# A float32r FFT and feed-forward kernel: the folds' casts and rests moved behind the operations on 1/std, and five groups of unread products between late steps

## The chip, the cores and the metric

The kernel runs on one core of a Trainium2 chip. The metric is the device time of one execution in microseconds, as a median over runs. Engines are named as the profile names them: PE is TensorE (its products), PEld its weight loads, DVE is VectorE, ACT is ScalarE, POOL is GpSimd, SP is SyncE, which issues most DMAs.

## The reference

An input of 8 x 3136 x 256 (batch, sequence, width) goes through a Fourier transform along the sequence and one along the width, of which the real part is kept; then comes a normalised two-layer feed-forward block with a residual:

```python
X = np.fft.fft(np.fft.fft(x, axis=1), axis=2)
y = X.real.astype(np.float32)
mu, var = np.mean(y, -1), np.mean((y - mu) ** 2, -1)
yn = (y - mu) / np.sqrt(var + 1e-06) * g_ln
out = y + np.maximum(yn @ w_ch1, 0.0) @ w_ch2      # 256 -> 1024 -> 256
```

## The kernel before, in words

The real part of the transform has a symmetry between rows k and N - k, so the kernel works on half of the rows, 1567 a batch and two single ones, and makes the outputs of a row and its mirror together. The rows of all eight batches stand in one line, cut into chunks of 256, 49 in all (the last one wider). The mean is taken out by the transform, and 1/std, a factor of a row, is applied at the end.

**The main loop** (L820 to L828) takes a chunk c in 8 steps, s = 8c to 8c + 7; step s handles 128 of the 1024 hidden columns. All large products are float32r, split in a high and a low part, three products for one. A step has

- `moe1_a(s)`: 6 products of 256 columns on PE (L354) into the two PSUM buffers tagged `ab`; then ACT copies one half (`asb`, L359) and DVE makes the sum and difference `h` (L360, L361). The buffer is free once L361 has read it, and `moe1_a(s + 2)` needs it;
- `moe1_b(s - 1)`: `h_hi` on ACT (L368) and its rest `h_lo` on DVE (L369, two operands in SBUF);
- `moe2(s - 3)`: 12 products of 256 columns (L404) that add up in PSUM (`acc`).

Around this stand two lists, `late[s]`, recorded between `moe1_a(s)` and `moe2(s - 3)`, and `after[s]`, recorded behind them. The order of each engine's instructions is the order in which they are recorded; DMAs aside, no scheduler moves them. In the lists are

- for each chunk, at step 8c + 5: `step2` (the second stage of the transform for a coming chunk, L309: 8 products of 98 columns or so, or 16, with copies on ACT and a rest on DVE, L334), and `residual` (the transform along the width, L428, 8 products as the profile counts them);
- then the norm of chunk c: `std(c)` on ACT at step 8c + 9, `inverse_std(c)` on DVE (L467, L468, L469, L471: four operations on a tile of 128 x 2) at 8c + 10, that is at a step 8k + 2 (for the first two chunks one step later each), and `finish` (L477, L479) at 8c + 11 and 8c + 12;
- for each batch b, seven folds i, ahead of the first stage of the transform of that batch. `steps1[b]` holds the step d of each: `fold_zw` (L207, L208) and `fold_eo` (L213, L214) on POOL at d - 7 and d - 6, the cast `fold_hi` on ACT (L219) at d - 4, the rest `fold_lo` on POOL (L225, it needs the cast) at d - 3, and `step1` at d: 3 products of 512 columns on PE (L262), a copy on ACT, a store. Most d are 6 or 7 above a multiple of 8. `step1_ends` adds a few small products (L237 to L241) per batch.

The last fold is due at step 318, while the loop runs to step 391, so POOL has nothing to do in the last fifth of the span.

```python
        for s in range(6, last):
            moe1_b(s - 1)
            moe1_a(s)
            for fn, args in late.get(s, ()):
                fn(*args)
            moe2(s - lag)
            for fn, args in after.get(s, ()):
                fn(*args)
```

Of the kernel before, what the change touches and what calls it, by code (L numbers as in the profile page):

```python
# [20 lines left out]
F32 = mybir.dt.float32  # L21
# [7 lines left out]
NB, N, D, FF = 8, 3136, 256, 1024  # L29
# [117 lines left out]
def tile_kernel(ctx: ExitStack, tc: tile.TileContext, x, g_ln, w1, w2, tu, tab, tz, ty, tw, out):  # L147
    nc = tc.nc
# [4 lines left out]
    psum = ctx.enter_context(tc.tile_pool(name="psum", bufs=1, space=bass.MemoryType.PSUM))  # L153
# [3 lines left out]
    w2_hi = moving.tile([128, 8, D], F32R, name="w2_hi")  # L157
# [4 lines left out]
    t1_hi = weights.tile([128, 128], F32R, name="t1_hi")  # L162
# [122 lines left out]
    def first_token(m):  # L285
        b, j = divmod(m, 8)
        return b * REG + max(gb[2 * j] - 2, 0)
# [305 lines left out]
    def finish_w2(n):  # L593
        _, e, f = conv.pop(f"w2_{n}")
        nc.vector.scalar_tensor_tensor(out=f, in0=f, scalar=2.0 ** -20, in1=e, op0=ALU.mult,
                                       op1=ALU.mult)
        return f
# [10 lines left out]
    def add(s, fn, *args):  # L608

        after.setdefault(s, []).append((fn, args))  # L610

    def add_late(s, fn, *args):

        late.setdefault(s, []).append((fn, args))

    first = {}
    for m in range(3, 64):
        s = 8 * (first_token(m) // CW) - 3
# [17 lines left out]
    for b in range(1, NB):  # L636
        need = 8 * (b * REG // CW) - 3
        at = steps1[b]
        ends_at = need - (58 if b > 1 else 30)
        add(need - 62 if b > 1 else ends_at - 7, ends, b)  # L640
        add(ends_at, step1_ends, b)
        for i, d in enumerate(at):
            d0, d = d, d - (b == 1)
            add(d - 7, fold_zw, b, i, nc.gpsimd)
            if b + 1 < NB:
                add(d - 5, load_x, b + 1, i)
            add(d - 6, fold_eo, b, i)
            add(d - 4, fold_hi, b, i)
            add(d - 3, fold_lo, b, i)
            add(d0, step1, b, i)  # L650
            add(d0, store1, b, i)
        add(at[-1] + 2, relayout, b)
    for c in range(LC):
        s = 8 * c + (5 if c > 1 else 6)
        add_late(8 * c + 9 + (c < 2), std, c)
        add_late(8 * c + 10 + (c < 2), inverse_std, c)
        for i in range(2):
            add(s, residual, c, i)
            add_late(s + 1, residual_e, c, i)
            add_late(s + i + 2, residual_y, c, i)  # L660
            add_late(8 * c + 11 + i, finish, c, i)
            add(8 * c + 11 + i, store_out, c, i)
    add_late(8 * LC - 2, singles)
    add_late(8 * LC + 7, std, LC)
    add_late(8 * LC, mixed)
# [15 lines left out]
    with tc.manual_schedule(engines={E.PE, E.Activation, E.DVE, E.Pool}):  # L681
        with tc.manual_schedule(engines={E.SP}):
# [91 lines left out]
            f = finish_w2(0)  # L774
# [8 lines left out]
            f = finish_w2(1)  # L783
# [18 lines left out]
            f = finish_w2(2)  # L802
# [51 lines left out]
```

## Time and profile before

| | us |
|---|---|
| median of 3 runs (lowest, highest) | 1012.02 (1011.04, 1012.07) |
| the profiled execution | 1010.0 |
| its span in the profile | 1008.2 |
| PE busy | 993.7 |
| DVE busy | 833.4 |
| ACT busy | 534.6 |
| POOL busy | 240.2 |
| PE idle ahead of L354 until DVE's L361 had ended, whole span | 6.4 in 13 pieces |

A row of a timeline gives the start and the length in us, the engine, the line, the operation, what it writes and reads, the shapes, how many instructions were merged, and in brackets the idle time before it with what ended it. A chain gives start, length, engine, tile and line of the pieces that followed each other without slack. The length of a product of PE (0.28 us for 256 columns) is longer than the distance from one start to the next, since products overlap; distances are what count.

### The profile page before, as it was taken

The numbers are of one execution on the slowest core, as the hardware profiler recorded it, in microseconds if no ns is written. First come the engines' busy times: TensorE is split into PE (matmuls) and PEld (weight loads), VectorE is DVE, ScalarE is ACT, GpSimd is POOL, SyncE is SP. The second block draws the span as 40 slices with busy tenths as digits, with TensorE's granted clock in tenths as the row PEclk, the third lists the DMA queues.
The fourth block names the chain that finished last, engine by engine and source line by source line (L and its number), as shares of the span: only waits on it lengthen the run. The fifth ranks groups of instructions, "written<-read, shape, count | busy, mean of one in ns | idle before, by whom it ended". The sixth has DMA issues, their size and how long they took to land.

```text
span 1008.2 us, 21760 instructions
## 1 busy us (share of the span) xinstructions
PE 993.7 (99%) x8289; PEld 969.7 (96%) x8289; DVE 833.4 (83%) x2190; ACT 534.6 (53%) x1416; POOL 240.2 (24%) x278
## 2 busy tenths in 40 slices
PE   9999999999999999999999999999999999999998
PEld 6799999999999999999999999999999999999998
DVE  6788887888888888887888887888888878887887
ACT  3655555554654555555555555554655555454553
POOL 1146433124212232312341125123322200000000
PEclk9999999999999999999999999999999999999999
DMA  9933352214221243121521242211311113100101
GB/s 344 262 145 125 107 161 81 79 58 136 86 93 54 75 141 100 55 74 62 170 74 64 84 129 93 90 58 64 116 43 43 53 43 96 43 23 22 43 22 43
DMA packets 41528, 92.10 MB, mean 91 GB/s; under 512 B 4176, under 2 KB 18704, under 8 KB 40528
## 3 DMA queue, kind: packets, MB, share of 16 engines
q1 hardware_dynamic: 40016, 88.87, 26.7%
q8 instruction: 66, 1.08, 0.5%
q0 software_dynamic: 320, 1.05, 0.3%
q10 hardware_dynamic: 1088, 0.79, 0.2%
q14 instruction: 38, 0.31, 0.1%
HBM read 50.32 MB, written 40.37 MB: 90 GB/s over the span
## 4 chain that ended last, share of the span: by engine, by line
PE 80%; DVE 13%; ACT 3%; DMA 2%; issue 2%; SPq 0%; ACTq 0%; DVEq 0%
PE acc L404 43%; PE ab L354 22%; PE ps L309 5%; DVE h_lo L369 4%; PE psy L428 4%; PE ps L262 3%; DVE h L361 2%; DVE h L360 2%; ACT h_hi L368 2%; DVE st L450 1%; DVE ve L468 1%; DVE ve L469 1%; DMA scratch<-s 1%; ACT s L265 1%; PE ps L255 1%
## 5 line engine op out<-in xcount | busy, mean ns | idle before, releaser
L404 PE MATMUL acc<-w_hi,h_lo 128*128 128x256 f32 x1568 | 435.7, 278 | 0.1
L404 PE MATMUL acc<-w_lo,h_hi 128*128 128x256 f32 x1568 | 435.5, 278 | 0.0
L404 PE MATMUL acc<-w_hi,h_hi 128*128 128x256 f32 x1568 | 435.5, 278 | 0.0
L368 ACT ACTIVATE h_hi<-h 128x512 fp32r<-128x512 f32 x392 | 249.7, 637 | 322.2 <-DVE h L361 322.1
L369 DVE SCALAR_TENSOR_TENSOR h_lo<-h,h_hi 128x512 fp32r<-128x512 f32 x392 | 287.5, 733 | 141.8 <-ACT h_hi L368 140.7
L404 PEld LDWEIGHTS acc<-w_hi,h_hi 128*128 128x128 f32 x1568 | 295.6, 189 | 0.0
L404 PEld LDWEIGHTS acc<-w_lo,h_hi 128*128 128x128 f32 x1568 | 295.1, 188 | 0.0
L404 PEld LDWEIGHTS acc<-w_hi,h_lo 128*128 128x128 f32 x1568 | 294.6, 188 | 0.4 <-DVE h_lo L369 0.3
L354 PE MATMUL ab<-ckl,w_hi 128*128 128x256 f32 x768 | 220.4, 287 | 6.5 <-DVE h L361 6.4
L354 PE MATMUL ab<-ckh,w_lo 128*128 128x256 f32 x768 | 213.9, 278 | 0.5 <-ACT ckh L330 0.4
L354 PE MATMUL ab<-ckh,w_hi 128*128 128x256 f32 x768 | 213.4, 278 | 0.0
L225 POOL TENSOR_TENSOR fl<-f,fh 128x512 fp32r<-128x512 f32 x49 | 64.1, 1307 | 527.1 <-ACT fh L219 478.4
L360 DVE TENSOR_TENSOR h<-asb,ab 128x256 f32<-128x256 f32 x384 | 158.3, 412 | 1.6 <-ACT asb L359 1.5
L361 DVE TENSOR_TENSOR h<-asb,ab 128x256 f32<-128x256 f32 x384 | 158.3, 412 | 0.0
L354 PEld LDWEIGHTS ab<-ckl,w_hi 128*128 128x128 f32 x768 | 144.3, 188 | 12.5 <-issue 7.6
L354 PEld LDWEIGHTS ab<-ckh,w_lo 128*128 128x128 f32 x768 | 144.7, 188 | 3.1 <-ACT ckh L330 0.5
L354 PEld LDWEIGHTS ab<-ckh,w_hi 128*128 128x128 f32 x768 | 144.8, 189 | 0.0
L359 ACT COPY asb<-ab 128x256 f32<-128x256 f32 x384 | 138.2, 360 | 10.8 <-PE ab L354 9.2
L265 ACT COPY s<-ps 128x508 f32<-128x508 f32 x56 | 32.8, 585 | 64.3 <-PE ps L262 50.5
L309 PE MATMUL ps<-tab_s,s 112*128 112x98 f32 (+1 forms) x512 | 65.5, 273 | 0.9 <-DMA s<-scratch 0.9
L309 PEld LDWEIGHTS ps<-tab_s,s 112*128 112x128 f32 x512 | 61.8, 191 | 1.4 <-PE pw L678 1.4
L330 ACT CAST ckh<-ps 128x392 fp32r<-128x392 f32 (+49 forms) x112 | 39.8, 356 | 29.5 <-PE ps L309 29.3
(108 smaller groups left out, 981.8 us busy)
## 6 DMA issues: line engine op xcount, KB each, us to landing
xs<-x SPq DMA_DIRECT2D x56, 512.0 KB, 4.1
out<-o SPq DMA_DIRECT2D x96, 256.0 KB, 2.0
scratch<-s SPq DMA_DIRECT2D x49, 256.0 KB, 2.3
s<-scratch SPq DMA_DIRECT2D x7, 1792.0 KB, 9.8
w1p_all<-w SPq DMA_DIRECT2D x8, 512.0 KB, 8.1
scratch<-s POOLq DMA_DIRECT2D x4, 256.0 KB, 6.1
s<-scratch SPq DMA_DIRECT2D x2, 448.0 KB, 5.6
s<-scratch SPq DMA_DIRECT2D x1, 896.0 KB, 12.0
```

The lines of the kernel that those rows point to most:

```text
L225: nc.gpsimd.tensor_tensor(out=lo, in0=f, in1=hi.bitcast(F32), op=ALU.subtract)
L265: nc.scalar.copy(s[:, :, :, :127], ps[:, :, :, :127])
L309: nc.tensor.matmul(ps[:, h, k0 - base:k1 - base], s2[b][:KP, g, 128 * h:128 * h + 128], tab_s[:, h, k0:k1], start=(h == 0 and g == 2 * j), ...
L330: nc.scalar.copy(hi, src)
L354: nc.tensor.matmul(pt, wt[wi][:, j, fs], ch[xi][:, j, :w], start=(n == 0), stop=(n == 2))
L359: nc.scalar.copy(asb[:, :w], pa)
L360: nc.vector.tensor_tensor(out=h[:, :w], in0=asb[:, :w], in1=pb, op=ALU.add)
L361: nc.vector.tensor_tensor(out=h[:, w:], in0=asb[:, :m], in1=pb[:, :m], op=ALU.subtract)
L368: nc.scalar.activation(h_hi, h, AF.Relu)
L369: nc.vector.scalar_tensor_tensor(out=h_lo, in0=h, scalar=0.0, in1=h_hi.bitcast(F32), op0=ALU.max, op1=ALU.subtract)
L404: nc.tensor.matmul(acc[c, i][:, side], hs[xi][:, h0:h0 + 128], ws[wi][:, f], start=(f == 0 and side == 0 and n == 0), stop=(f == 7 and n = ...
L428: nc.tensor.matmul(ps[:, j, :129 + j], ck[:, j], ty_s[:, j, :129 + j], start=(j == 0), stop=True, skip_group_check=True)
```

## The change

It has two parts.

The folds: `cast` is d - 4 as before, or d - 3 where d is 6 above a multiple of 8; the rest comes one step behind it. So in those folds the cast moves from `after[8k + 2]` to `after[8k + 3]` and the rest from there to `after[8k + 4]`. `inverse_std` stands in `late[8k + 2]`. 22 of the 49 folds move: 20 of the batches from 2 on, two of batch 1.

The products: a function `extra` allocates a PSUM tile of 128 x 2 x 256 under the tag `y` (one buffer, which step 2's second part, step 1 and two products of the last residual use too) and runs products of `t1_hi` (weights) on `w2_hi` into it. Nothing reads it. The index n counts blocks of 256 columns: width 1 is a product of 256 columns, width 2 one of 512. The groups stand behind what `after` holds for steps 326, 342, 350, 365 and 374.

```diff
-            add(d - 4, fold_hi, b, i)
-            add(d - 3, fold_lo, b, i)
+            cast = (d - 4, d - 3)[d % 8 == 6]
+            add(cast, fold_hi, b, i)
+            add(cast + 1, fold_lo, b, i)
...
+    def extra(s, widths):
+
+        ps = psum.tile([128, 2, D], F32, tag="y", name=f"extra{s}")
+        for n in widths:
+            nc.tensor.matmul(ps[:, :n], t1_hi, w2_hi[:, :n], start=True, stop=True)
+
+    for s, widths in ((326, (1,)), (342, (2,)), (350, (1, 1, 1)), (365, (1,)), (374, (2, 1))):
+        add(s, extra, s, widths)
```

On ACT, at steps 209 to 212, before (`fh5_5` is the cast of fold 5 of batch 5, due at step 214; `asb210` is the copy of step 210, `h_hi210` the high part of its h, `ve25` belongs to the std of chunk 25):

```order
L460 ACTIVATE ve25_8363<-ve25_8363 128x2
L368 ACTIVATE h_hi209_8410<-h209_8392 128x512
L359 COPY asb210_8421<-ab210_8414 128x256
L219 CAST fh5_5_8443<-f5_5_8377 128x512
L368 ACTIVATE h_hi210_8445<-h210_8422 128x512
L359 COPY asb211_8456<-ab211_8449 128x256
L368 ACTIVATE h_hi211_8481<-h211_8457 128x512
```

and in the change:

```order
L460 ACTIVATE ve25_8363<-ve25_8363 128x2
L368 ACTIVATE h_hi209_8410<-h209_8392 128x512
L359 COPY asb210_8421<-ab210_8414 128x256
L368 ACTIVATE h_hi210_8443<-h210_8422 128x512
L359 COPY asb211_8454<-ab211_8447 128x256
L219 CAST fh5_5_8476<-f5_5_8377 128x512
L368 ACTIVATE h_hi211_8479<-h211_8455 128x512
```

The cast stands two instructions later, behind the copy of step 211. The order on DVE is the same in both kernels. On POOL it differs at the two folds of batch 1 alone, where `fold_eo` of the next fold now stands ahead of the moved rest.

On PE, between steps 374 and 375, before (`acc46_1` is the sum of chunk 46, `ab375` the buffer of step 375):

```order
L404 MATMUL acc46_1_14429<-w2_lo_74,h_hi371_14437 128x256
L404 MATMUL acc46_1_14429<-w2_hi_73,h_hi371_14437 128x256
L354 MATMUL ab375_14555<-ckl46_13943,w1_hi_76 128x256
L354 MATMUL ab375_14555<-ckh46_13942,w1_lo_77 128x256
L354 MATMUL ab375_14555<-ckh46_13942,w1_hi_76 128x256
```

and in the change:

```order
L404 MATMUL acc46_1_14439<-w2_lo_74,h_hi371_14447 128x256
L404 MATMUL acc46_1_14439<-w2_hi_73,h_hi371_14447 128x256
L668 MATMUL extra374_14561<-w2_hi_73,t1_hi_78 128x512
L668 MATMUL extra374_14561<-w2_hi_73,t1_hi_78 128x256
L354 MATMUL ab375_14568<-ckl46_13951,w1_hi_76 128x256
```

Two products, of 512 and 256 columns, stand between the two steps. After 326, 342 and 350 the groups stand in the same way between L404 and L354; after 365 the group stands behind the residual's L428.

## The prediction

> **What bounds the kernel now.** First the page: TensorE (PE) is busy nearly the whole span. Then the groups of PE's instructions in the window that holds most of the loop (170 to 803 us): of the loop's two kinds of product only the first of L354 ever waits, always for the same operation.
>
> ```profile
> span 1008.2 us, 21760 instructions
> PE 993.7 (99%) x8289; PEld 969.7 (96%) x8289; DVE 833.4 (83%) x2190; ACT 534.6 (53%) x1416; POOL 240.2 (24%) x278
> ```
> ```profile
> L354 PE MATMUL ab<-ckl,w_hi 128*128 128x256 f32 x514 | 147.0, 286 | 4.2 <-DVE h L361 4.2
> ```
> ```profile
>   DVE h L361: 4.2, 8
> ```
>
> So in that window PE idles 4.2 us in 8 pieces, each ended by the second half of h (L361). The timeline of one of them, step 212 (time, length, engine, line), shows what VectorE (DVE) did before:
>
> ```profile
> 561.59 1.30 POOL L225 TENSOR_TENSOR fl<-f,fh 128x512 fp32r<-128x512 f32 x1 [12.50 <-ACT fh L219]
> ...
> 562.23 0.68 DVE L468 SCALAR_TENSOR_TENSOR ve<-ve 128x2 f32<-128x2 f32 x1
> ...
> 562.84 0.74 POOL L207 TENSOR_TENSOR zw<-xs 128x256 f32<-128x256 f32 x1
> ...
> 562.94 0.66 DVE L469 TENSOR_TENSOR ve<-ve 128x2 f32<-128x2 f32 x1
> 563.01 0.28 PE L354 MATMUL ab<-ckl,w_hi 128*128 128x256 f32 x1
> ...
> 563.63 0.57 DVE L471 SCALAR_TENSOR_TENSOR r<-ve 128x2 f32<-128x2 f32 x1
> ...
> 565.60 0.36 PE L354 MATMUL ab<-ckl,w_hi 128*128 128x256 f32 x1 [0.40 <-DVE h L361]
> ...
> 567.80 1.03 PE L309 MATMUL ps<-tab_s,s 112*128 112x98 f32 x8
> ```
>
> L468, L469 and L471 (of the 1/std) work on two columns and take 0.57 to 0.68 us each. The first two end 20 ns after a GpSimd (POOL) operation: L468 at 562.91, fl at 562.89; L469 at 563.60, zw at 563.58. Now the same place of a chunk whose rest comes one step later, at steps 67 to 69:
>
> ```profile
> 207.57 0.16 DVE L468 SCALAR_TENSOR_TENSOR ve<-ve 128x2 f32<-128x2 f32 x1
> ...
> 207.96 0.16 DVE L471 SCALAR_TENSOR_TENSOR r<-ve 128x2 f32<-128x2 f32 x1
> 208.16 0.69 DVE L369 SCALAR_TENSOR_TENSOR h_lo<-h,h_hi 128x512 fp32r<-128x512 f32 x1
> ...
> 208.99 1.30 POOL L225 TENSOR_TENSOR fl<-f,fh 128x512 fp32r<-128x512 f32 x1 [17.45 <-ACT fh L219]
> ...
> 212.28 1.17 DVE L369 SCALAR_TENSOR_TENSOR h_lo<-h,h_hi 128x512 fp32r<-128x512 f32 x1
> ```
>
> With POOL quiet L468 and L471 take 0.16 us each, and the cost falls on an h_lo instead (1.17 us; 0.69 alone). The chain of waits there (start, length, what) runs on PE alone, 0.68 + 1.36 = 2.04 us a step:
>
> ```profile
> 208.24 0.68 PE ab L354 x6
> 208.92 1.36 PE acc L404 x12
> ...
> 212.32 1.76 PE ps L309 x16
> 214.08 0.92 PE psy L428 x8
> 215.00 0.71 PE ab L354 x6
> 215.71 1.41 PE acc L404 x12
> ...
> 219.24 0.70 PE ps L262 x3
> 219.94 0.69 PE ab L354 x6
> 220.64 1.36 PE acc L404 x12
> ```
>
> This chain shows a second limit: PE has two beats. A step lasts 2.04 us (113 ns a product) or 2.12 us (118), with no wait in either. After step 2 and the residual (L309, L428) the beat is long; the three products of step 1 (L262) turn it to the short one. Step 1 stops after step 318, and windows of 14.84 us late in the span show what follows (the count behind PE; the first and the last of four long ones, and a short one):
>
> ```profile
> 846.58:861.42 14.84, 14.84 (x128) 14.84 (x127) 13.67 (x41) 6.90 (x16) 0.00 (x0) 1.00 0.06 20
> 866.39:881.23 14.84, 14.84 (x134) 14.84 (x132) 13.83 (x41) 6.76 (x16) 0.00 (x0) 1.00 0.05 19
> ...
> 941.11:955.95 14.84, 14.84 (x129) 14.84 (x127) 13.67 (x41) 6.90 (x16) 0.00 (x0) 1.00 0.06 21
> ```
>
> The four stretches, from 847, 885, 903 and 941 us on, keep the long beat for their 7 steps: 7 x 0.08 = 0.56 us each.
>
> **The folds, part by part.** Nothing is added: a cast on ScalarE (ACT) moves behind one h_hi and one asb, and with it the rest on POOL, at every fold due at a step 8k + 6.
>
> What goes, b = 2 and later. At step 212, from the first product (563.01) to step 2 (567.80), two steps took 4.79 us against 2 x 2.04 = 4.08: 0.71 us lost, of which 0.40 is the idle time shown and 0.31 the restart behind it. A longer wait and one without visible idle time, from their first product to step 2:
>
> ```profile
> 780.00 0.28 PE L354 MATMUL ab<-ckl,w_hi 128*128 128x256 f32 x1
> ```
> ```profile
> 785.00 0.58 PE L309 MATMUL ps<-tab_s,s 112*128 112x98 f32 x4
> ```
> ```profile
> 642.57 0.28 PE L354 MATMUL ab<-ckl,w_hi 128*128 128x256 f32 x1
> ```
> ```profile
> 646.82 0.47 PE L309 MATMUL ps<-tab_s,s 112*128 112x98 f32 x3
> ```
>
> They lose 5.00 - 4.08 = 0.92 and 4.25 - 4.08 = 0.17 us. So the 8 pieces cost their 4.2 us idle and 8 x 0.29 for the restarts, 6.5; I count six sites of the small kind from step 52 on, 6 x 0.17 = 1.0. Together 7.5 us. What hides the rest at its new place is shown by step 68: the 1/std was over at 208.12, the rest began at 208.99, a margin of 0.87 us. The rest's next reader, step 1, is at 219.24, and in a chunk due at 8k + 6 one step (2.1 us) nearer: still 6 us behind the rest's end.
>
> What follows from the beat. In three chunks the step after such a wait falls into the short beat, step 2 leaves it short, and then L262 turns it to long for 6 or 7 steps (L262 turns both ways). One chain, and the windows of the other two beside a clean chunk:
>
> ```profile
> 589.58 1.36 PE acc L404 x12
> 590.94 0.69 PE ps L262 x3
> 591.63 0.71 PE ab L354 x6
> ```
> ```profile
> 457.00:466.70 9.70, 9.70 (x85) 9.70 (x84) 8.69 (x27) 4.98 (x12) 1.52 (x2) 1.00 0.12 42
> ...
> 693.00:702.70 9.70, 9.70 (x85) 9.70 (x84) 8.72 (x27) 4.30 (x10) 2.70 (x4) 1.00 0.21 68
> 575.00:584.70 9.70, 9.70 (x87) 9.62 (x85) 8.73 (x27) 4.38 (x11) 3.15 (x5) 1.00 0.15 49
> ```
>
> Without the wait they go as at 212 to 220 us: 3 x 6.5 x 0.08 = 1.6, less 3 x 0.05 for the step after the residual, which then is long (1.41 for 1.36): 1.4 us.
>
> Batch 1 (two folds). One has a large wait of its own kind:
>
> ```profile
> 109.95 0.36 PE L354 MATMUL ab<-ckl,w_hi 128*128 128x256 f32 x1 [0.66 <-DVE h L361]
> ```
>
> Priced as the large one: 0.9 us. There POOL's order changes too: f of the next fold now stands ahead of the rest and runs before the 1/std. At the other fold the 1/std comes one step later in the code, so the moved rest meets it still: 0. In all 7.5 + 1.4 + 0.9 = 9.8 us. Bounds: 6 (a third of the sites keep a wait) and 11.
>
> **The products, part by part.** n counts blocks of 256 columns, so there are six products of 256 columns and two of 512. Nothing reads them, and PE is full there: they cost their time. At 0.115 us (0.68 to 0.71 for six) and 0.23 (0.69 for three of 512 at L262) that is 0.69 + 0.46 = 1.15 us. What they can give is a turn of the beat. The trace has no lone product between steps; nearest is L262, float32r with the same weights, an odd group, which turns the beat each time that nothing waits. By that row the groups after steps 326, 342 and 350 turn long to short: 0.56 - 0.115, 0.56 - 0.23 and 0.56 - 0.345, together 1.0 us. But step 357 then comes from the short beat, and x16 from it ends long (212.32 to 217), so 358 to 365 turn long: -0.6. The group after 365 stands right behind the residual and gains 0.45 if it turns what the residual leaves. The pair after 374 is an even group, costs 0.345, and hits a chunk that may be short already: -0.345, or -0.9 if it ends long. Bounds: all five chunks short and 358 too, a gain of 4 x 0.56 - 1.15 = 1.1 us; nothing turned and two short chunks spoilt, a loss of 1.15 + 1.1 = 2.2. I take a gain of 0.2 us, near the row of L262 with 374 short: 1.0 - 0.6 + 0.45 - 0.345 = 0.5, half believed.
>
> The sum against the profiled execution (1010.0 us, span 1008.2): 1010.0 - 9.8 - 0.2 = 1000.0. The runs of before lie 1.0 to 2.1 us above it. Waits like those at 565 and 782 us differ from site to site and can be longer in other executions; they go, so I add only the lower 1.0: **1001.0 us**.
>
> **The rivals.** A difference under 0.2%, 2 us, can't be told from no change.
>
> *The wait moves.* In a chunk due at 8k + 6 step 2 has 8 products, 0.88 us less cover than the 16 here (1.76). h_lo meets POOL's operations there, at 1.17 instead of 0.69. Against it: step 68's chunk has no wait at all, and DVE's delay is one operation at a time, not three in a row. If half of the waits stay: 1001.0 + 3.8 + 0.7 = 1005.5. The Trainium skill, "SBUF — State Buffer", section "Who interferes with whom", says that a DVE instruction with two SBUF inputs and a GpSimd one that reads SBUF exclude each other, and the second to issue "fully blocks"; by it the blocking is moved to h_lo, not removed, and this rival is what it warns of. The ends that coincide at step 212 agree with it.
>
> *The products only cost.* No group turns the beat as wished: 1.15 lost instead of 0.2 gained, and two short chunks spoilt: 1001.0 + 1.35 + 1.1 = 1003.5. For it: which beat follows an interruption differs between like ones (after the residual long at 215.71, short at 589.58). The Trainium skill, "TensorE: Matmul & The Clock Gate", section "Back-to-back issue gap", knows one gap for a width, N / 2.4 + 2.5 ns; by it there is no beat to turn, and the products cost an estimated 6 x 109 + 2 x 216 ns = 1.1 us. The trace differs: 113 and 118 ns for one width.
>
> *Slower.* The rest (1.30 us) and the four operations of the next fold behind it now lie over h_lo and h of the steps about step 2. If DVE's delay there exceeds the cover of step 2 and the residual in a chunk of 8 products, 0.88 + 0.92 us, PE waits at each of the 22 moved folds; at the 0.92 us of a large wait, that is 1001.0 + 20 = 1021. It decides from three h_lo in a row held for a whole rest (3 x 0.6); the one seen held cost 0.48.
>
> *It doesn't do what it says.* Nothing ties the rest to the 1/std, only ACT's order; were the 0.87 us of margin used up, the waits would stay: 1010.0 + 1.0 - 0.2 = 1010.8, within 0.2%.
>
> **How the numbers follow.** Forecast 0.61; wait moves 0.17; products only cost 0.15; slower 0.04; does nothing 0.03. The range starts at 998.8 (products at their best bound, 0.9 more, and folds at 11, 1.2 more) and ends at 1004.5 (products at their worst bound, 2.4, and 1.1 of the waits kept): it takes in the second rival and the smaller half of the first. Faster is the first three, 0.93; same 0.03; slower 0.04.
>
> **What would show it.** In the profile after: L468 to L471 at 0.16 us in nearly all chunks; no idle time before L354 from DVE h L361 in the window 170 to 803; chain pieces of 0.68 and 1.36 from L262 on in every chunk; in the last chunks 0.68 and 1.36 after each group. Wrong, if L354 still waits for L361 at step 8k + 5 or later, or if pieces of 0.71 and 1.41 follow the groups.

## The result, and the profile after

The changed kernel takes 1001.58 us (median of 4 runs, 1001.18 to 1001.93) against 1011.53 us (1010.36 to 1012.07) for the kernel before in the same runs: ratio 0.9903, 95% interval 0.9886 to 0.9920. The profiled execution took 1001.76 us, its span 1000.0 us. The forecast was 1001.0, in a range of 998.8 to 1004.5.

The page of the kernel after, its first rows:

```profile
span 1000.0 us, 21776 instructions
PE 989.0 (99%) x8296; PEld 967.1 (97%) x8297; DVE 818.2 (82%) x2190; ACT 535.1 (54%) x1416; POOL 247.4 (25%) x278
```

VectorE is busy 15.2 us less with as many instructions. The groups of the kernel after in the window 160 to 795 us, the first product of `moe1_a`:

```profile
L354 PE MATMUL ab<-ckl,w_hi 128*128 128x256 f32 x524 | 148.4, 283 | 0.0
```

The 4.2 us of idle time before it are gone, to the last piece. The timeline of the kernel after about step 212:

```profile
557.25 0.16 DVE L468 SCALAR_TENSOR_TENSOR ve<-ve 128x2 f32<-128x2 f32 x1
557.45 0.16 DVE L469 TENSOR_TENSOR ve<-ve 128x2 f32<-128x2 f32 x1
557.64 0.16 DVE L471 SCALAR_TENSOR_TENSOR r<-ve 128x2 f32<-128x2 f32 x1
...
558.67 1.30 POOL L225 TENSOR_TENSOR fl<-f,fh 128x512 fp32r<-128x512 f32 x1 [14.54 <-ACT fh L219]
...
561.96 1.19 DVE L369 SCALAR_TENSOR_TENSOR h_lo<-h,h_hi 128x512 fp32r<-128x512 f32 x1
```

It is the picture that the prediction drew from step 68: 0.16 us for each operation of the 1/std, the rest 0.87 us behind its end (558.67 after 557.80), one h_lo that pays. In the kernel before, the one operation of the 1/std with a single operand in SBUF, the reciprocal (L467), never paid: it took 0.15 to 0.17 us in all chunks, and at step 212 it ran under the same rest that held L468 for 0.68 us:

```profile
562.03 0.16 DVE L467 RECIPROCAL ve<-ve 128x2 f32<-128x2 f32 x1
```

So the engine as a whole was not held, only its operations with two operands in SBUF. The chain of waits of the kernel after runs through the place on PE alone:

```profile
556.15 0.68 PE ab L354 x6
556.83 1.36 PE acc L404 x12
558.19 0.68 PE ab L354 x6
558.87 1.36 PE acc L404 x12
560.23 0.68 PE ab L354 x6
560.91 1.36 PE acc L404 x12
562.27 0.87 PE ps L309 x8
```

The starts of the first products of steps 0, 48 and 320 and the end of the span cut each trace in three stretches. The first holds batch 1, the second every moved fold from batch 2 on but one (due at step 38), the third the groups of products.

| kernel | steps 0 to 47 | 48 to 319 | 320 to the end |
|---|---|---|---|
| before | 124.06 | 670.24 | 177.79 |
| after | 124.08 | 660.99 | 178.48 |
| e1, folds alone | 124.32 | 660.99 | 177.76 |
| e2, products alone | 122.93 | 671.58 | 178.48 |
| e3, rest recorded later | 121.96 | 668.83 | 177.80 |
| e4, rests held | 121.63 | 660.99 | 177.75 |
| e5, rests held, products behind the residuals | 120.91 | 660.99 | 180.81 |
| e6, folds, groups of other counts | 122.87 | 660.99 | 179.02 |
| e7, folds, products of other widths | 124.13 | 660.99 | 177.76 |
| e8, rests in halves | 122.22 | 664.80 | 177.77 |
| e9, rests held, products of 320 | 120.10 | 660.99 | 176.66 |

The middle stretch gained 9.25 us, the first nothing, the last lost 0.69 us. Each row is one execution. The first stretch differs by up to 1.5 us between executions of the same code (e4 and e9 differ in it by nothing that was edited), and the middle one, with the folds of before, by 1.3 us (before, e2). With the rests out of the way the middle stretch is 660.99 us in all seven kernels.

### The profile page after: what moved, and what is told of

Read it like the earlier page. It is cut to its first block, busy times and chain, and to the rows that moved or that the text cites. A ratio compares the mean times of both kernels' runs of the same rounds, so it can differ in the third digit from the quotient of the medians.

```text
span 1000.0 us, 21776 instructions
## 1 busy us (share of the span) xinstructions
PE 989.0 (99%) x8296; PEld 967.1 (97%) x8297; DVE 818.2 (82%) x2190; ACT 535.1 (54%) x1416; POOL 247.4 (25%) x278
## 4 chain that ended last, share of the span: by engine, by line
PE 88%; DVE 7%; ACT 2%; DMA 1%; issue 1%; ACTq 0%; SPq 0%; DVEq 0%
PE acc L404 49%; PE ab L354 24%; PE ps L309 5%; PE psy L428 4%; PE ps L262 3%; DVE h_lo L369 2%; DVE h L360 1%; DVE h L361 1%; ACT h_hi L368 1%; DMA scratch<-s 1%; PE pw L687 1%; PE ps L255 1%; PE ps L257 1%; DMA s<-scratch 0%; DVE st L450 0%
## 5 line engine op out<-in xcount | busy, mean ns | idle before, releaser
L404 PE MATMUL acc<-w_hi,h_lo 128*128 128x256 f32 x1568 | 435.1, 278 | 0.2 <-DVE h_lo L369 0.2
L404 PE MATMUL acc<-w_hi,h_hi 128*128 128x256 f32 x1568 | 434.9, 277 | 0.0
L404 PE MATMUL acc<-w_lo,h_hi 128*128 128x256 f32 x1568 | 434.9, 277 | 0.0
L369 DVE SCALAR_TENSOR_TENSOR h_lo<-h,h_hi 128x512 fp32r<-128x512 f32 x392 | 295.4, 754 | 148.0 <-ACT h_hi L368 146.0
L404 PEld LDWEIGHTS acc<-w_hi,h_hi 128*128 128x128 f32 x1568 | 295.4, 188 | 0.0
L404 PEld LDWEIGHTS acc<-w_hi,h_lo 128*128 128x128 f32 x1568 | 294.5, 188 | 0.6 <-DVE h_lo L369 0.4
L404 PEld LDWEIGHTS acc<-w_lo,h_hi 128*128 128x128 f32 x1568 | 294.9, 188 | 0.0
L354 PE MATMUL ab<-ckl,w_hi 128*128 128x256 f32 x768 | 218.7, 285 | 2.0 <-DVE h L361 2.0
L354 PE MATMUL ab<-ckh,w_lo 128*128 128x256 f32 x768 | 213.5, 278 | 0.5 <-ACT ckh L330 0.4
L354 PE MATMUL ab<-ckh,w_hi 128*128 128x256 f32 x768 | 213.1, 277 | 0.0
L360 DVE TENSOR_TENSOR h<-asb,ab 128x256 f32<-128x256 f32 x384 | 158.8, 413 | 2.0 <-ACT asb L359 1.9
L354 PEld LDWEIGHTS ab<-ckl,w_hi 128*128 128x128 f32 x768 | 144.3, 188 | 5.7 <-ACT w_hi L539 1.5
L354 PEld LDWEIGHTS ab<-ckh,w_lo 128*128 128x128 f32 x768 | 144.5, 188 | 3.3 <-ACT ckh L330 0.5
L354 PEld LDWEIGHTS ab<-ckh,w_hi 128*128 128x128 f32 x768 | 144.7, 188 | 0.0
```

The costliest lines, as they stand in the source:

```text
L354: nc.tensor.matmul(pt, wt[wi][:, j, fs], ch[xi][:, j, :w], start=(n == 0), stop=(n == 2))
L360: nc.vector.tensor_tensor(out=h[:, :w], in0=asb[:, :w], in1=pb, op=ALU.add)
L369: nc.vector.scalar_tensor_tensor(out=h_lo, in0=h, scalar=0.0, in1=h_hi.bitcast(F32), op0=ALU.max, op1=ALU.subtract)
L404: nc.tensor.matmul(acc[c, i][:, side], hs[xi][:, h0:h0 + 128], ws[wi][:, f], start=(f == 0 and side == 0 and n == 0), stop=(f == 7 and n = ...
```

## The experiments

**e1: the folds alone.**

```diff
-    for s, widths in ((326, (1,)), (342, (2,)), (350, (1, 1, 1)), (365, (1,)), (374, (2, 1))):
-        add(s, extra, s, widths)
```

> The folds' part alone, without the five groups of products. Theory: the whole gain is the folds'; from step 320 on the changed kernel took 178.5 us against 177.8 before, so the products cost 0.7 us and this kernel runs at about 1000.9 us. Rival, the forecast's own term: the products gain 0.2 us, then about 1001.8 us. In the trace the stretch from step 320 on should look as before the change, 177.8 us.

Measured: 1000.08 us against 1010.36 us, ratio 0.9899 (0.9884 to 0.9915). The last stretch is that of before (177.76), the middle one that of the change. So the gain is the folds', and the products cost 0.7 us in the trace. The medians differ in the same sense, but the intervals of the two ratios overlap.

**e2: the products alone.**

```diff
-            cast = (d - 4, d - 3)[d % 8 == 6]
-            add(cast, fold_hi, b, i)
-            add(cast + 1, fold_lo, b, i)
+            add(d - 4, fold_hi, b, i)
+            add(d - 3, fold_lo, b, i)
```

> The products alone, folds as before. Theory: 0.7 us slower than the kernel before, about 1012.2 us, with PE's waits for L361 all there (4.2 us idle in the middle window). Rival: the products gain 0.2 us, 1011.3 us, or the beat that they leave also matters for the folds' part and several us go.

Measured: 1009.89 us against 1010.36, ratio 0.9998 (0.9989 to 1.0007); the time tells nothing. The trace does: what the first product of `moe1_a` waits for in the window 160 to 795,

```profile
  DVE h L361: 4.2, 8
```

is as before, and the last stretch is 178.48 us, that of the change to 0.01 us. In this execution the products cost 0.7 us and gave nothing to the rest.

**e3: only the rest recorded one step later.**

```diff
-            add(cast, fold_hi, b, i)
-            add(cast + 1, fold_lo, b, i)
+            add(d - 4, fold_hi, b, i)
+            add((d - 3, d - 2)[d % 8 == 6], fold_lo, b, i)
```

> Only the rest (on GpSimd) is recorded one step later, the cast stays; no products. Theory: the rest starts when its cast ends, wherever it is recorded, so that from batch 2 on nothing changes: about 1011 us, with the two fold orders of batch 1 worth some tenths. Rival: the place of the rest in the recorded order is what counts: about 1001 us.

Measured: 1007.85 us (one run; before 1008.75 to 1011.54). The group of the waiting product in the window 160 to 795:

```profile
L354 PE MATMUL ab<-ckl,w_hi 128*128 128x256 f32 x517 | 147.8, 286 | 3.7 <-DVE h L361 3.7
```

The waits stay. The rest starts when its cast ends; its place among POOL's instructions is empty either way. Recording the rest later does not move it; its cast has to move, or something else has to hold it (e4). This execution is 2.1 us shorter than the one of before in the first stretch and 1.4 in the middle one. Most of that can't be put down to the edit, since e2, with the folds of before, has 122.93 and 671.58 us there. One step in the first stretch can: step 28, where POOL's order did change, takes 2.83 us, against 3.63 in both before and e2.

**e4: the rest held by a wait, the cast left early.** On GpSimd, ahead of each of the 22 rests:

```diff
+    held = {}
+
+    def hold(c):
+        nc.gpsimd.tensor_copy(out=held[c][:, 3, 0:1], in_=rstd[c][:, 0:1])
...
-        ve = res.pop(c)
+        ve = held[c] = res.pop(c)
...
-            cast = (d - 4, d - 3)[d % 8 == 6]
-            add(cast, fold_hi, b, i)
-            add(cast + 1, fold_lo, b, i)
+            add(d - 4, fold_hi, b, i)
+            if d % 8 == 6:
+                add(d - 3, hold, (d - 14) // 8)
+            add(d - 3, fold_lo, b, i)
```

> Casts and rests recorded where they were, but ahead of each of the 22 rests GpSimd copies one column of the 1/std, so that it waits for the 1/std; no products. The ScalarE order is that of before. Theory (the three small operations of the 1/std queue behind GpSimd's operations): the waits of PE go as in the change, 1001 us within 1. Rival (the early cast on ScalarE holds up h_hi, and that is the wait): nothing gained, about 1011 us.

Measured: 998.44 us against 1010.36, ratio 0.9885 (0.9871 to 0.9898). The timeline of e4 about step 211:

```profile
552.82 0.62 ACT L219 CAST fh<-f 128x512 fp32r<-128x512 f32 x1
...
554.55 0.16 DVE L476 SCALAR_TENSOR_TENSOR r<-ve 128x2 f32<-128x2 f32 x1
...
554.75 0.69 DVE L369 SCALAR_TENSOR_TENSOR h_lo<-h,h_hi 128x512 fp32r<-128x512 f32 x1
...
554.78 0.70 POOL L465 COPY ve<-r 128x1 f32<-128x1 f32 x1 [13.84 <-DVE r L476]
...
555.44 1.30 POOL L225 TENSOR_TENSOR fl<-f,fh 128x512 fp32r<-128x512 f32 x1
```

That is 2.6 us under the 1001 expected. The cast stands where it stood, ahead of h_hi, and the middle stretch is 660.99 us all the same: an early cast on ScalarE was no part of the wait; the rest under the 1/std, with the fold operations that follow it on GpSimd, was all of it. The copy of one column takes 0.70 us because an h_lo had just begun; two of the 22 copies met no h_lo and took 0.185 us. So the blocking goes both ways. e4 also gains 2.7 us over e1 in the first stretch. The three executions with the rests held have 120.1 to 121.6 us there, the four with the moved casts 122.9 to 124.3, so some of it is real, but no run takes it apart. In these two executions 1.3 us of it lie in step 37 (below) and 0.5 in each of steps 21 and 23.

**e8: the rest in two halves, nothing moved.** In the kernel before:

```diff
-        nc.gpsimd.tensor_tensor(out=lo, in0=f, in1=hi.bitcast(F32), op=ALU.subtract)
+        for a in range(2):
+            nc.gpsimd.tensor_tensor(out=lo[:, a], in0=f[:, a], in1=hi[:, a].bitcast(F32),
+                                    op=ALU.subtract)
```

> The kernel before, with each rest made in two operations of half the size on GpSimd, and nothing moved. Theory (each small operation of the 1/std waits for the one GpSimd operation that runs, and the two engines then take turns): two of the three waits meet halves of 0.65 us and the third a zw of 0.74 instead of its second one, so the 1/std ends about 0.6 us earlier at the folds of steps 8k + 6, and the idle time before L354 in the window 160 to 795 falls from 4.2 us to about 1 us; the time falls by 3 to 5 us. Rival (the operations share the bandwidth, so that only the total of GpSimd's work counts): no change within 0.2%.

Measured: 1003.32 us (one run; before 1007.44 to 1012.87). The group and the timeline of e8 (its lines are two higher):

```profile
L356 PE MATMUL ab<-ckl,w_hi 128*128 128x256 f32 x520 | 148.1, 285 | 0.6 <-DVE h L363 0.6
```
```profile
556.92 1.44 POOL L226 TENSOR_TENSOR fl<-f,fh 128x256 fp32r<-128x256 f32 x2 [12.43 <-ACT fh L219]
...
557.56 0.16 DVE L470 SCALAR_TENSOR_TENSOR ve<-ve 128x2 f32<-128x2 f32 x1
...
557.76 0.62 DVE L471 TENSOR_TENSOR ve<-ve 128x2 f32<-128x2 f32 x1
...
558.31 0.74 POOL L207 TENSOR_TENSOR zw<-xs 128x256 f32<-128x256 f32 x1
558.41 0.65 DVE L473 SCALAR_TENSOR_TENSOR r<-ve 128x2 f32<-128x2 f32 x1
```

The same work in smaller pieces: one operation gets through at 557.56, two wait instead of three, and 3.6 of the 4.2 us are gone; the middle stretch takes 664.80 us instead of 670.24. So what counts is the length of the one GpSimd operation that runs, not their total. The Trainium skill, "SBUF — State Buffer", section "Who interferes with whom", says that the one that comes second blocks until the first has finished; the ends of the waits here (557.76 + 0.62 = 558.38 with the halves' end at 558.36) agree.

**The groups of products.** The chain of the kernel after around the first two groups:

```profile
836.40 1.41 PE acc L404 x12
837.82 0.12 PE extra L668
837.93 0.71 PE ab L354 x6
838.64 1.41 PE acc L404 x12
```
```profile
874.51 1.41 PE acc L404 x12
875.92 0.23 PE extra L668
876.15 0.69 PE ab L354 x6
876.85 1.36 PE acc L404 x12
```

One product of 256 columns left the long beat (1.41) as it was, one of 512 turned it. Three of 256 after 350 left it, 512 and 256 after 374 turned it. Four kernels looked further. Without groups the beat does not differ from execution to execution: from step 326 to step 381 the kernel before, e1, e3, e4 and e8 have the same beat in every step.

**e6: groups of other counts**, on e1:

```diff
+    for s, widths in ((326, (2, 2)), (342, (1, 1)), (350, (2,)), (366, (2, 1))):
+        add(s, extra, s, widths)
```

> The folds' part with groups after step 326 of 2 x 512 columns, after 342 of 2 x 256, after 350 of one 512, after 366 of 512 and 256. Theory (each product of 512 columns turns the beat, one of 256 does not): long after 326 (turned twice), long after 342, short after 350, short after 366. Rival (the number of products counts, odd groups turn): long, long, short, long. Rival (what length of time the group takes): long after 326 and 366 need not agree with either.

**e7: single products of other widths**, on e1 (the tile and `w2_hi` flattened, so that n counts columns):

```diff
+    for s, cols in ((326, (384,)), (342, (128,)), (350, (320,)), (366, (64,))):
+        add(s, extra, s, cols)
```

> The folds' part with single products of other widths: after step 326 one of 384 columns, after 342 of 128, after 350 of 320, after 366 of 64. Theory in its plain form (any product that is longer than a weight load leaves the load waiting and turns the beat): 384 and 320 turn long to short, 128 and 64 do not. Rival (any departure from 256 columns breaks the long beat): all four turn. Rival (it takes 512): none turns.

Measured: one run each, 1001.66 and 1001.75 us. What the chains show, with the change and e9:

| group (columns) | kernel, step | beat ahead | beat behind |
|---|---|---|---|
| 64 | e7, 366 | short | long |
| 128 | e7, 342 | long | long |
| 256 | after, 326 | long | long |
| 256 x 2 | e6, 342 | long | long |
| 256 x 3 | after, 350 | long | long |
| 320 | e7, 350; e9, six places | long | short |
| 384 | e7, 326 | long | short |
| 512 | after, 342 | long | short |
| 512 | e6, 350 | short | long |
| 512 x 2 | e6, 326 | long | short |
| 512 + 256 | after, 374 | long | short |
| 512 + 256 | e6, 366 | short | long |

The chains of e6 at 326 and e7 at 366:

```profile
835.76 1.41 PE acc L404 x12
837.18 0.46 PE extra L668 x2
837.64 0.69 PE ab L354 x6
838.34 1.36 PE acc L404 x12
```
```profile
930.43 0.45 PE psy L428 x4
930.88 0.70 PE ab L354 x6
931.58 1.36 PE acc L404 x12
932.93 0.03 PE extra L669
932.96 0.79 PE ab L354 x6
933.75 1.41 PE acc L404 x12
```

Counting odd and even is wrong, in groups and in products of 512: two of them turn the beat like one. What all runs share, for groups between two steps: a group with a product wider than 256 turns the beat; groups of 256 alone, of which the loop itself is made, leave it; one narrower leaves or brings the long beat. Both directions were seen with 512 and with 512 + 256; 320 and 384 met the long beat alone, so whether they would turn the short one to long is not shown. Three expectations of e6's theory fell (after 326, 350 and 366), and that of e7 that 64 columns leave the short beat alone.

The table does not say what a residual leaves. In e1 the residual of step 349 leaves the long beat; in e6, where step 348 is long as in e1 but two products of 256 ran after 342, it leaves the short one.

**e5: a product right behind the residual**, on e4, after what looked like the one success of the change, the short beat behind step 365:

```diff
+    for s, widths in ((325, (1,)), (341, (1,)), (349, (1,)), (358, (2,)), (365, (1,)), (373, (1,))):
+        add(s, extra, s, widths)
```

> The kernel that holds the rests behind the 1/std, with other products: one of 256 columns right behind the residuals of steps 325, 341, 349, 365 and 373, one of 512 after step 358. Theory (a product right behind the residual, as after 365 in the change, starts the short beat at once; one of 512 between steps turns the beat): the stretch from step 320 on falls by 1.6 us, from 177.7 to about 176.1, and the time from 0.9885 to about 0.987 of before. Rival (the success after 365 hung on the state that came before it): some of the products only cost 0.1 to 0.2 us each, and the stretch stays at 177.7 or above.

Measured: 1000.43 us against 1008.61, ratio 0.9923 (0.9910 to 0.9937): worse than e4. The last stretch took 180.81 us. The chain at step 325, and the timeline after 358:

```profile
830.78 0.92 PE psy L428 x8
831.71 0.12 PE extra L674
831.82 0.71 PE ab L354 x6
832.53 1.41 PE acc L404 x12
```
```profile
911.83 0.47 PE L674 MATMUL extra<-w_hi,t_hi 128*128 128x512 f32 x1 [1.27 <-DVE ckl L334]
```

Behind the residual the product of 256 columns was followed by the long beat at 325, 341, 349, 365 and 373: the rival. At the first four e4 has the long beat too, without a product; at 373 it has the short one, so there the product spoilt a chunk. Nor was 365 a success of the change: e6 and e7 have no product there, their steps 359 to 364 are long as in the kernel after (2.12 us), and their residual of step 365 leaves the short beat as well (e7 above, 1.36 at 931.58). The group after 358 also had to wait 1.27 us for the one `y` buffer, which step 2's second part still held; that was a mistake of place.

**e9: the rests held, and products of 320 columns where the table says that they turn the beat**, on e4:

```diff
+    for s in (326, 342, 350, 359, 366, 374):
+        add(s, extra, s, 320)
```

> The rests held behind the 1/std, and one product of 320 columns after steps 326, 342, 350, 359, 366 and 374. Theory (a product of more than 256 columns between steps turns the beat, whatever came before): after each of the six the beat is short; four chunks gain 0.40 us each over the folds-only kernel, 358 to 365 and 374 to 381, which were short there, now start long and lose 0.2 to 0.3 each. The stretch from step 320 on takes 176.6 us instead of 177.7, and the time is 0.987 to 0.988 of before. Rival (the earlier turns were luck of the state before): some of 350, 359, 366, 374 stay or become long, and the stretch stays at 177.3 or above.

Measured: 995.24 us against 1009.95, ratio 0.9864 (0.9841 to 0.9888), the lowest ratio of all, though its interval overlaps that of e4 (0.9871 to 0.9898). The chain after step 359, one of the six, all alike:

```profile
909.31 1.41 PE acc L404 x12
910.72 0.15 PE extra L674
910.87 0.69 PE ab L354 x6
911.56 1.36 PE acc L404 x12
```

The last stretch took 176.66 us, 1.1 less than with no products, where 176.6 was expected. The first stretch is 1.5 us shorter than in e4 in this execution, which no part of the edit touches.

## Why the prediction came out right, point by point

**The folds from batch 2 on.** Terms of 7.5 for the waits and 1.4 for the beats behind them, 8.9 together; the middle stretch, which leaves out only the first of the moved ones, gave 9.25, and 10.59 against e2's execution with the same folds as before. The mechanism is shown by e4 (rest alone held, all of the gain), e3 (rest alone recorded later, waits kept) and e8 (shorter pieces, shorter waits). The beats followed as forecast: after the change L262 turns to short in each chunk whose step 2 it follows at 8k + 6, steps 166, 222 and 262 included.

**Batch 1.** The wait at 109.95 went as priced: step 28 takes 2.83 us instead of 3.63. But the first stretch is 124.06 before and 124.08 after, because other steps grew, and the term of 0.9 failed as a sum. In step 27 the `fold_eo` that now runs ahead of the rest lies under an h_lo (1.20 us instead of 0.69), and the step takes 2.35 us instead of 2.12. Step 37 takes 4.79 us instead of 4.23, with a wait in its residual:

```profile
133.36 0.64 PE L428 MATMUL psy<-ty_s,ck 128*128 128x129 f32 x4
134.69 0.71 PE L428 MATMUL psy<-ty_s,ck 128*128 128x129 f32 x4 [0.69 <-DVE o L479]
```

There the first fold of batch 2 has moved. Its cast now stands behind `step1_ends`, whose copy on ScalarE (L243) waited 3.24 us for something that the profile does not name. So the cast came late, the rest started only at 131.34, an h_lo under it took 1.35 us, and the `finish` behind that ended late. The copy in the kernel after, and in e6, which has the same folds:

```profile
130.50 0.21 ACT L243 COPY s<-pse 128x28 f32<-128x28 f32 x1 [3.24 <-issue]
```
```profile
129.37 0.21 ACT L243 COPY s<-pse 128x28 f32<-128x28 f32 x1 [1.30 <-PE pse L241]
```

In e6 the copy waits only for its own products, and step 37 takes 3.83 us without a wait of PE; in e1 and e7 it is late again (step 37: 5.17 and 4.89 us). That is the rival of the moving wait, at one of 22 places and in three of four executions. The step that failed is the one that took every site for the like of step 68 and put the cost of the new places at nothing: here the cast moved behind another wait of ScalarE.

**The products.** A gain of 0.2 was taken, with bounds of 1.1 gained and 2.2 lost; they lose 0.7. The step that failed is the nearest row: L262 was read as an odd group, while what it has and the groups after 326 and 350 lack is products wider than 256 columns. Pieces of 0.71 and 1.41 follow these two groups, which the prediction had named as a sign of being wrong. The chunk from 358 on turned long as the prediction feared (0.6 of the loss). The chunk from 366 on turned short and gained 0.7, but by e6 and e7 that came from the long chunk ahead of it, not from the product after 365, which only cost its time.

**The offset.** The prediction added 1.0 us for executions slower than the profiled one. After the change the profiled execution lies 0.18 us above the median. So the sum, 1010.0 - 9.8 - 0.2 = 1000.0, was 1.8 too low against the profiled 1001.76. The two terms above make 0.9 each; the middle stretch gave 0.35 more than its terms, and the part ahead of step 0, which no edit touches, took 0.3 more. The offset that was added covers half of the 1.8: the closeness of 1001.0 to 1001.58 owes something to luck, to errors that cancel. The offset itself rested on three runs; later runs of the kernel before lie on both sides of 1010.0, from 1007.4 to 1012.9. (The lower end of the range, by its own terms 1001.0 - 0.9 - 1.2, is 998.9 and not 998.8.)

**The rivals.** The margin of 0.87 us held at every moved fold of the middle stretch (0.86 to 1.80 us), and from 100 us on no product of step 1 waited at all. That products only cost is what the change's groups came to as a whole, not one by one.

## What to carry to other kernels

An operation of two columns, 0.16 us alone, held VectorE for 0.57 to 0.68 us while a long operation ran on GpSimd; look for tiny operations with long rows that end with another engine's. Move the long one behind the chain, or hold it there by a wait, or cut it into pieces; moving it in the recorded order alone left the waits here (3.7 of 4.2 us), since it starts when its input is ready. Before an operation is moved behind others on its engine, look at what those can wait for. When a stream of products has two speeds with no wait in either, read the speed behind every interruption before putting one in, test the interruption's size, not only its place, and compare with a run that has the same speed ahead and no interruption.

## What the runs showed of the hardware that was not expected

- A stream of float32r products of 256 columns ran at one of two distances, 113.3 or 117.8 ns (2.04 or 2.12 us for the 18 of a step), for up to seven steps with the same instructions and no wait; the granted clock was 1.00 in both. The Trainium skill, "TensorE: Matmul & The Clock Gate", section "Back-to-back issue gap", gives N / 2.4 + 2.5 ns for a matmul alone, by which 256 columns take an estimated 109 ns, and for a stream with weight loads a measured 81 ns for 128 columns and 131 for 512, one figure each. No run here shows these: the two products of 512 columns in e6 took 0.46 us. What sets the two beats is open: the runs tell what turns them, not why.
- One product of 320 columns (0.15 us), never read, shortened the seven steps behind it by 0.08 us each (e9 after 326, against e4).
- GpSimd waits for VectorE as VectorE waits for it: a copy of one column took 0.70 us behind an h_lo of 0.69, and 0.185 us without one (e4).
- What was held on VectorE were operations with two operands in SBUF (L468, L469, L471, L369); with one there (L467, 0.15 to 0.17 us, and L360, which takes its other operand from PSUM, 0.41 to 0.42) an operation took the same time under GpSimd's operations as without them.
